# Block-sparse attention and MoE: row maxima by pairs of 64-row matmuls, the mask added on VectorE, tokens in natural order

## The chip, the cores and the metric

The kernel runs on one core of one Trainium2 chip. The time is the device time in microseconds of one execution. A core has five engines with queues of their own: TensorE (PE, matmuls, with its weight loads shown apart as PEld), VectorE (DVE), ScalarE (ACT), GpSimd (POOL) and SyncE (SP), which here issues nearly all DMAs. TensorE writes its results to PSUM, eight banks of 512 fp32 numbers for each of 128 partitions; all else lies in SBUF.

## What is computed

Four batches of eight heads, 768 tokens, 64 numbers a head. Attention is masked by blocks of 32 tokens: a query block sees its neighbours, the first and the last block, and three sampled blocks; the first and last query blocks see all. Then two matrix products with an activation between them.

```python
scores = scale * np.matmul(q, k.transpose(0, 1, 3, 2))
...
scores = np.where(mask, scores, -1000000000.0)
scores = scores - np.max(scores, axis=-1, keepdims=True)
attn = np.exp(scores)
attn = attn / (np.sum(attn, axis=-1, keepdims=True) + 1e-09)
return np.matmul(attn, v)
...
h = x @ w_in                      # x: 3072 x 512, w_in: 512 x 2048
g = np.where(pos, h, np.where(neg, 0.0, (h + beta) ** 2 / (4.0 * beta)))
return g @ w_out                  # 2048 x 512
```

Queries and keys are scaled by 8, so the scores are large and the maximum of each row has to be taken off before the exponential.

## The kernel before

**Precision.** TensorE works on fp32 numbers in a rounded form (F32R). Where that is too coarse, a number is split into a rounded high part and a rounded rest, and three products of the four are summed: in the scores (the rest terms in a second matmul, L304), in the values from head 10 on (L335, L336; heads 0 to 9 multiply whole fp32 numbers, L333), and in both MoE layers (L457 to L459, L485 to L487).

**One head** (`head`, L198). The host gives q and k with the 64 numbers of a token along the partitions and the tokens along the columns, in an order where column t*128 + p is token 6p + t (`_columns`, L596, and the mask's indicator rows `ind`, L586, in the same order). `load_qk` brings q and k of a head into one tile of 128 partitions (q in the lower half L, k in the upper half R). `hi` (L216) rounds it on ScalarE, `lo` (L227) takes the rest on VectorE. Then four DMAs on SP's queue move the halves: `hi_one` (L223) fills rows 0-63 of KA and QA; `hi_two` (L230) and `lo_two` (L236) fill the two halves of QB and KB, which hold a high part and a rest each, arranged so that one matmul of 128 rows sums both mixed products.

QA and KA have more rows than these 64: rows 64 to 87 carry the mask (KA: which block a column belongs to; QA: 0 or -2^33 for each key block, made once by `consts`, L119 to L124), rows 96 to 101 carry the row maximum (KA: ones; QA: minus the maximum of the query). So one matmul gives scores with the mask added, and the score matmul of 102 rows (L303) also takes the maximum off.

**The maxima.** For each of six query tiles t and each half kh of the keys, `max_mm` (L263) multiplies 88 rows (q times k, and the mask) into a PSUM bank of 128 queries x 384 keys, and `max_red` (L271) lets VectorE take the maximum over the 384 into a column of `mc`. Twelve such pairs of matmul and reduction make a head. `max_col` (L276) joins the halves, `max_turn` (L280) transposes the six columns on TensorE, and `max_row` (L283) writes them, negated, into QA's rows 96 to 101.

**Scores to values.** For each half of the queries and each of six key tiles: `scores` (two matmuls), `expo` on ScalarE (L308), a split of p (L196 on ScalarE, L316 on VectorE), running sums on GpSimd (L323), and `values`. Then come the denominators, their reciprocals and the products that make x for the MoE.

**Banks.** The eight PSUM banks are `pa` (three buffers), `po`, `hp` and `oa0` to `oa2`. In the first batch's eight heads (`wide`) the MoE does not run yet, and the scores take `oa0`, `oa1` and `hp` in turn while the maxima take `pa` (`RINGS`, L567). From head 8 on scores, maxima, transposes and sums share the three `pa`.

**Order.** Every step is put into a list with a due time by `at(t, ...)`. The unit is a slot, one score tile: 12 slots a head. Offsets come from tables (P, PW, PA; L555 to L565): the moves are due `qs` slots before the head's scores (12.454 for the first batch, 11.825 for the second, 9.647 then), the maxima `m0` (about 7.8) before them and spread over `m1` (5 to 5.6) slots, each reduction `mr` (0.06 to 0.46) after its matmul. The list is sorted (L545) and the program issued in that order, each engine working through its own part in order. The weights of the two MoE layers are converted on the fly from their 64-bit form in the first stages (`convert`, L157, on ScalarE and VectorE), and the MoE of one batch (`moe`, L434) runs beside the attention of the next. The MoE's output is stored by three tiles at once, or for the last one tile by tile (L490 to L504).

Of the kernel before, what the change touches and what calls it, by code (L numbers as in the profile page):

```python
# [8 lines left out]
F32 = mybir.dt.float32  # L9
# [4 lines left out]
ALU = mybir.AluOpType  # L14
AX = mybir.AxisListType
# [3 lines left out]
B, H, S, D = 4, 8, 768, 64  # L19
NB, BLK, NR = 24, 32, 3  # L20
T = 6
HALF = 384
# [5 lines left out]
KM = 64 + NB  # L28
# [9 lines left out]
def body(ctx, tc, qk_t, v, sampled_blocks, moe_w_in, moe_w_out, ind, cm, negd, ident, fold, out):  # L38
    nc = tc.nc
    pool = lambda name, bufs, **kw: ctx.enter_context(tc.tile_pool(name=name, bufs=bufs, **kw))  # L40
    cst = pool("cst", 1)
    ld = pool("ld", 1)
    tp = pool("tp", 1)
    qk = pool("qk", SETS)
    vp = pool("vp", 2)
    pp = pool("pp", 3)
# [8 lines left out]
    psa = pool("psa", 3, space=PSUM)  # L55
# [5 lines left out]
    Q_MOVE = nc.sync  # L61
# [9 lines left out]
    Q_V = nc.sync  # L71

    def f(ap):
        return ap.bitcast(F32)
# [8 lines left out]
    KAt = [cst.tile([128, S], F32R, name=f"KA{i}") for i in range(SETS)]  # L83
    VW = [vp.tile([128, T, 128], F32, name="vn") for _ in range(2)]
    wi = cst.tile([128, 4, 2, FF], F32R, name="wi")

    def consts():
        M = slice(64, KM)
        for i in range(SETS):
            nc.gpsimd.memset(f(QA[i][64:128 if i == 0 else 96]), 0.0)  # L90
        nc.gpsimd.memset(VW[0][:, :, 64:128], 1.0)
        nc.gpsimd.memset(VW[1][:, :, 0:64], 1.0)
        nc.vector.memset(eps, 1e-9)
        nc.vector.memset(half_c, 0.5)
        sraw = cst.tile([128, NR, 2], I32, name="sraw")
        nc.sync.dma_start(out=sraw[M], in_=sampled_blocks.bitcast(I32).rearrange("a (r w) -> a r w", w=2))
        cmt = cst.tile([128, 2 * NB], F32, name="cmt")
        nc.sync.dma_start(out=cmt[M], in_=cm)
        ef = f(cv.tile([128, 512, 2], I32, name="raw", bufs=3).rearrange("p c w -> p (c w)"))[64:KA, 0:S]
        nc.sync.dma_start(out=ef, in_=ind)  # L100
        idf = pp.tile([128, HALF], F32, name="pt")[:, 0:128]
        nc.sync.dma_start(out=idf, in_=ident)
        nc.vector.tensor_copy(out=idr, in_=idf)
        nc.vector.tensor_copy(out=KAt[0][64:KA], in_=ef)
        nc.sync.dma_start(out=nd, in_=negd.rearrange("a (t p) -> a t p", t=T))
        nc.sync.dma_start(out=sel, in_=fold)
        for i in range(1, SETS):
            rounded(nc.gpsimd, KAt[i][64:KA], ef)
        sf = cst.tile([128, NR], F32, name="sf")
        nc.vector.tensor_copy(out=sf[M], in_=sraw[M, :, 0])  # L110
        al = cst.tile([128, NB], F32, name="al")
        nc.vector.tensor_copy(out=al[M], in_=cmt[M, 0:NB])
        for r in range(NR):
            nc.vector.scalar_tensor_tensor(
                out=al[M], in0=cmt[M, NB:2 * NB], scalar=sf[M, r:r + 1], in1=al[M],
                op0=ALU.is_equal, op1=ALU.max)
        mb = cst.tile([128, NB], F32R, name="mb")
        nc.vector.tensor_scalar(out=mb[M], in0=al[M], scalar1=-1.0, scalar2=BIG, op0=ALU.add, op1=ALU.mult)
        for hf in range(2):  # L119
            cs = slice(hf * HALF, (hf + 1) * HALF)  # L120
            pm = psa.tile([128, 512], F32, name="pa")
            nc.tensor.matmul(out=pm[0:NB, 0:HALF], lhsT=mb[M], rhs=KAt[0][64:KM, cs], start=True, stop=True)
            for i in range(SETS):
                (nc.scalar.copy if i else nc.vector.tensor_copy)(out=QA[i][64:KM, cs], in_=pm[0:NB, 0:HALF])  # L124
# [4 lines left out]
    def at(t, fn, *args):  # L129
        plan.append((t, fn, args))  # L130
# [3 lines left out]
    def bank(wide, use="s"):  # L134

        if wide:
            ring = RINGS[use]
            n = turns[use] = turns.get(use, -1) + 1
            name = ring[n % len(ring)]
            if name[0] == "o":  # L140
                return psc.tile([128, DM], F32, name=name)
            if name == "hp":
                return psh.tile([128, 512], F32, name="hp")
        return psa.tile([128, 512], F32, name="pa")
# [43 lines left out]
    L, R = slice(0, 64), slice(64, 128)  # L188

    def rounded(eng, dst, src):  # L190
        if eng is nc.vector:
            eng.tensor_copy(out=dst, in_=src)
        elif eng is nc.gpsimd:
            eng.tensor_scalar(out=dst, in0=src, scalar1=1.0, scalar2=0.0, op0=ALU.mult, op1=ALU.add)
        else:
            eng.copy(out=dst, in_=src)  # L196

    def head(i, n0, b, h, pst):  # L198

        j, e = divmod(h, 2)  # L200
        wide = i < H
        whole = i // 2 in WHOLE
        G = {**P, **PW} if wide else {**P, **PA} if i < 2 * H else P
        o0, o1 = (L, R) if e == 0 else (R, L)
        QAi, KAi = QA[i % SETS], KAt[i % SETS]
        st = {}

        def load(n, src):
            t = st[n] = ld.tile([128, T, D], F32, name=n)
            Q_V.dma_start(out=t, in_=src[b, h].rearrange("(p t) d -> p t d", t=T))  # L210

        def load_qk():
            st["x"] = ld.tile([128, S], F32, name="qk")
# [6 lines left out]
        def move(dst, src):  # L220
            Q_MOVE.dma_start(out=f(dst), in_=f(src))
# [8 lines left out]
        def hi_two():  # L230
            st["KB"] = qk.tile([128, S], F32R, name="KB")
            st["QB"] = qk.tile([128, S], F32R, name="QB")
            move(st["QB"][L], st["hi"][L])
            move(st["KB"][R], st["hi"][R])

        def lo_two():  # L236
            Q_MOVE.dma_start(out=f(st["QB"][R]), in_=st["x"][L])
            Q_MOVE.dma_start(out=f(st["KB"][L]), in_=st["x"][R])

        def split(pl, n, src, hi, lo):  # L240
            t = st[n] = pl.tile([128, T, 128], F32R, name="vn")
# [7 lines left out]
        pre = n0 - EARLY  # L249
        at(-99 if i == 0 else pre - G["qs"] - G["ld"], load_qk)  # L250
        at(n0 - G["vs"] - G["ld"], load, "lv", v)
        if whole:
            at(n0 - G["vw"], v_whole)
# [2 lines left out]
        at(pre - G["qs"] - 0.4, hi)  # L256
        at(pre - G["qs"] + 0.2, hi_one)
        at(pre - G["qs"] + 0.4, lo)
        at(pre - G["qs"] + 1.3, hi_two)
        at(pre - G["qs"] + 1.6, lo_two)  # L260


        def max_mm(t, kh):  # L263
            if "mc" not in st:
                st["mc"] = pr.tile([128, T, 2], F32, name="mc", bufs=2)
            pm = bank(wide, "m")
            nc.tensor.matmul(out=pm[:, 0:HALF], lhsT=QAi[0:KM, t * 128:(t + 1) * 128],  # L267
                             rhs=KAi[0:KM, kh * HALF:(kh + 1) * HALF], start=True, stop=True)
            st["pm", t, kh] = pm

        def max_red(t, kh):  # L271
            nc.vector.reduce_max(out=st["mc"][:, t, kh:kh + 1], in_=st.pop(("pm", t, kh))[:, 0:HALF], axis=AX.X)  # L272

        def max_col(lo=0, n=T):
            mr = st["mr"] = pr.tile([128, T], F32R, name="mr", bufs=2)
# [8 lines left out]
                                    in0=st["pr"][0:n, 0:128].unsqueeze(1).to_broadcast([n, n - lo, 128]),  # L284
                                    in1=nd[0:n, lo:n], op=ALU.mult)

        jobs = [(t, kh) for t in range(T) for kh in range(2)]
        for n, (t, kh) in enumerate(jobs):
            u = pre - (G["m0"] - G["m1"] * n / len(jobs))
            at(u, max_mm, t, kh)  # L290
            at(u + G["mr"], max_red, t, kh)
        if i == 0:
            for d, fn in ((-0.9, max_col), (-0.89, max_turn), (-0.88, max_row)):
                at(pre - (G["m0"] - G["m1"] / 2) + G["mr"] + H0 + d, fn, 0, T // 2)
# [103 lines left out]
        for hf in range(2):  # L398
# [9 lines left out]
            u = s - 1 + G["lag"]  # L408
# [25 lines left out]
    def moe(t0, p, b, hf, first):  # L434

        g = {}
        G = {**P, **PM} if first else P
# [49 lines left out]
            nc.tensor.matmul(out=o, lhsT=gl[:, ts], rhs=w[:, 0], start=False, stop=(fi == NF - 1))  # L487

        end = b == B - 1 and hf == 1
        dst = out[b * S:(b + 1) * S].rearrange("(p t) m -> p t m", t=T)  # L490

        def o_copy(t):
            if t == 0:
# [12 lines left out]
        for fi in range(NF):  # L506
            u = t0 + fi * p
# [7 lines left out]
            m = u + p / 2  # L515
# [10 lines left out]


    at(TC, consts)
    for i in range(NHEADS):
        b, h = divmod(i, H)  # L530
        if h % 2 == 0:
            pst = {}
        head(i, PER * i, b, h, pst)
    begin = [PER * H * (b + 1) + DELAY for b in range(B + 1)]
    p = PER * H / (2 * NF)
# [39 lines left out]
CONV, CSTEP = 8.0, 5.75  # L575
CLO, CHI = (struct.unpack("<f", struct.pack("<I", w))[0] for w in (0x38100000, 0x47EFFFFF))

_INS = ["qk_t", "v", "sampled_blocks", "moe_w_in", "moe_w_out"]
_OUTS = [((B * S, DM), "float32")]


def _constants():
    import numpy as np

    col = np.arange(S)
    block = (T * (col % 128) + col // 128) // BLK  # L586
    ind = np.concatenate([block[None, :] == np.arange(NB)[:, None], np.zeros((8, S)), np.ones((T, S))]).astype(np.float32)
    i, j = np.arange(NB)[:, None], np.arange(NB)[None, :]
    base = (abs(i - j) <= 1) | (i == 0) | (j == 0) | (i == NB - 1) | (j == NB - 1)
    cm = np.concatenate([base.astype(np.float32), np.broadcast_to(j, (NB, NB)).astype(np.float32)], axis=1)  # L590
    negd = -(np.arange(S)[None, :] // 128 == np.arange(T)[:, None]).astype(np.float32)
    return {"ind": ind, "cm": np.ascontiguousarray(cm), "negd": np.ascontiguousarray(negd),
            "ident": np.eye(128, dtype=np.float32), "fold": np.tile(np.eye(32, dtype=np.float32), (4, 1))}


def _columns(_np, a):  # L596

    return a.reshape(B, H, 128, T, D).transpose(0, 1, 4, 3, 2).reshape(B, H, D, S)


# [27 lines left out]
```

## Time and profile before

| | |
|---|---|
| time, three runs | 981.95, 982.35, 989.32 us (median 982.35) |
| profiled execution | 983.67 us, span 981.8 us |
| busy: TensorE matmul / weight loads | 942.5 us (96%) / 828.1 us (84%) |
| busy: VectorE / ScalarE / GpSimd | 747.5 us (76%) / 636.5 us (65%) / 251.8 us (26%) |
| matmuls and weight loads | 4687 each, 384 of them for the maxima (L267) |
| granted TensorE clock | 0.998 |
| DMA | 154.43 MB, mean 157 GB/s |

The span goes from the first to the last instruction. A matmul's end is modelled and matmuls follow each other in a pipeline, so their durations overlap and a busy TensorE isn't the same as a TensorE at its limit: the pace is read from the starts. A row of a group has the line, the engine, the operation, the tile written and the tiles read, the shapes and the count, then busy time and the mean duration of one in ns, then the idle time before these instructions and what ended it. A row of a timeline has the start in us, the duration in us, the engine, the line and the operation. A row of windows has the stretch, its length, and busy time with count for each engine, then the granted clock, the DMA share and GB/s.

### The profile page before, as it was taken

How to read it: one execution, taken by the hardware profiler on the slowest of the kernel's cores; microseconds unless marked ns; L12 is line 12 of the kernel's file. 1: busy time of each engine (PE TensorE's matmuls, PEld its weight loads, DVE VectorE, ACT ScalarE, POOL GpSimd, SP SyncE). 2: the span in 40 equal slices, each digit the busy share in tenths (PEclk: the TensorE clock that was granted, in tenths of full speed). 3: DMA queues.
4: the chain of work that ended last, by engine and by line, in shares of the span. 5: the costliest groups of instructions: out<-in, count | busy, mean ns of one | idle time of the engine just before them, and what ended most of it. 6: DMA issues, size and time to landing. Idle time of an engine off the chain costs nothing.

```text
span 981.8 us, 14556 instructions
## 1 busy us (share of the span) xinstructions
PE 942.5 (96%) x4687; PEld 828.1 (84%) x4687; DVE 747.5 (76%) x1403; ACT 636.5 (65%) x1302; POOL 251.8 (26%) x229
## 2 busy tenths in 40 slices
PE   5899899999889999999999999999999999999998
PEld 3666677877779899999989998998999999899997
DVE  5888999889998888978788888888888885422222
ACT  3667777677667676767677767776767676433433
POOL 1000000023334343433434343343434343000000
PEclk9999999999999999999999999999999999999999
DMA  6756677754355444645555443645445432433432
GB/s 195 205 149 189 196 209 225 259 180 139 123 182 163 145 143 133 182 139 153 159 150 182 131 150 116 199 137 175 138 142 178 125 115 89 154 130 129 160 129 97
DMA packets 56216, 154.43 MB, mean 157 GB/s; under 512 B 9612, under 2 KB 17952, under 8 KB 56140
## 3 DMA queue, kind: packets, MB, share of 16 engines
q1 hardware_dynamic: 56100, 153.48, 51.5%
q8 instruction: 37, 0.61, 0.3%
q14 instruction: 39, 0.32, 0.1%
q10 hardware_dynamic: 40, 0.03, 0.0%
HBM read 100.92 MB, written 14.81 MB: 118 GB/s over the span
## 4 chain that ended last, share of the span: by engine, by line
PE 85%; DVE 7%; ACT 3%; DMA 2%; issue 2%; SPq 0%; ACTq 0%; DVEq 0%
PE oa L485 8%; PE oa L487 8%; PE oa L486 8%; PE hp L457 8%; PE hp L459 7%; PE hp L458 7%; PE pa L267 7%; PE pa L303 5%; PE pa L304 5%; PE po L335 5%; PE po L336 4%; PE po L333 4%; DVE mc L272 2%; PE oa L333 2%; DMA QA<-qkh 1%
## 5 line engine op out<-in xcount | busy, mean ns | idle before, releaser
L323 POOL TENSOR_TENSOR acc<-acc,pt 128x384 f32<-128x384 f32 x176 | 201.7, 1146 | 233.0 <-ACT pt L308 195.1
L272 DVE TENSOR_REDUCE mc<-pa 128x1 f32<-128x384 f32 x384 | 202.5, 547 | 19.3 <-PE pa L267 16.1
L196 ACT CAST ph<-pt 128x384 fp32r<-128x384 f32 x264 | 135.5, 514 | 92.4 <-PE po L335 89.3
L316 DVE TENSOR_TENSOR pl<-pt,ph 128x384 fp32r<-128x384 f32 x264 | 163.6, 620 | 34.7 <-ACT ph L196 34.0
L308 ACT ACTIVATE pt<-pa 128x384 f32<-128x384 f32 x288 | 140.6, 489 | 54.6 <-PE pa L304 45.0
L457 PE MATMUL hp<-x,wi 128*128 128x384 f32 x448 | 155.5, 347 | 4.0 <-DVE r L469 4.0
L485 PE MATMUL oa<-w,gh 128*128 128x512 f32 x384 | 153.3, 399 | 0.3 <-ACT gh L196 0.3
L487 PE MATMUL oa<-w,gl 128*128 128x512 f32 x384 | 151.6, 395 | 0.3 <-DVE gl L478 0.3
L459 PE MATMUL hp<-x,wi 128*128 128x384 f32 x448 | 151.2, 338 | 0.0
L458 PE MATMUL hp<-x,wi 128*128 128x384 f32 x448 | 151.1, 337 | 0.0
L486 PE MATMUL oa<-w,gh 128*128 128x512 f32 x384 | 150.8, 393 | 0.0
L267 PE MATMUL pa<-KA,QA 88*128 88x384 f32 x384 | 138.3, 380 | 5.4 <-DMA QA<-qkh 3.8
L323 POOL TENSOR_TENSOR acc<-pt 128x384 f32<-128x384 f32 x44 | 46.5, 1058 | 345.5 <-ACT pt L308 345.5
L469 DVE SCALAR_TENSOR_TENSOR r<-r,hp 128x384 f32<-128x384 f32 x112 | 61.5, 549 | 73.3 <-ACT r L466 72.9
L478 DVE TENSOR_TENSOR gl<-r,gh 128x384 fp32r<-128x384 f32 x128 | 84.3, 658 | 24.0 <-ACT gh L196 23.5
L303 PE MATMUL pa<-QA,KA 102*128 102x384 f32 x288 | 99.0, 344 | 1.8 <-ACT pt L308 1.1
L463 ACT ACTIVATE r<-hp,half_c 128x384 f32<-128x384 f32 x112 | 65.1, 582 | 54.1 <-PE hp L459 51.2
L304 PE MATMUL pa<-QB,KB 128*128 128x384 f32 x288 | 97.9, 340 | 0.0
L267 PEld LDWEIGHTS pa<-KA,QA 88*128 88x128 f32 x384 | 73.1, 192 | 28.7 <-DVE mc L272 4.7
L335 PE MATMUL po<-ph,vn 128*128 128x384 f32 x264 | 91.4, 346 | 5.1 <-DVE xun L345 3.4
L457 PEld LDWEIGHTS hp<-x,wi 128*128 128x128 f32 x448 | 84.5, 189 | 10.7 <-DVE r L469 6.1
L336 PE MATMUL po<-pl,vn 128*128 128x384 f32 x264 | 88.6, 336 | 0.0
(97 smaller groups left out, 1624.3 us busy)
## 6 DMA issues: line engine op xcount, KB each, us to landing
w<-wo_dram SPq DMA_DIRECT2D x112, 512.0 KB
qk<-in_qk_t_dram SPq DMA_DIRECT2D x32, 384.0 KB
raw<-in_moe_w_in_dram SPq DMA_DIRECT2D x16, 512.0 KB
raw<-in_moe_w_out_dram SPq DMA_DIRECT2D x16, 512.0 KB
wo_dram<-w SPq DMA_DIRECT2D x16, 512.0 KB
lv<-in_v_dram SPq DMA_DIRECT2D x32, 192.0 KB
KA<-qkh SPq DMA_DIRECT2D x32, 192.0 KB
QA<-qkh SPq DMA_DIRECT2D x32, 192.0 KB
```

Source lines behind the costliest of these rows:

```text
L267: nc.tensor.matmul(out=pm[:, 0:HALF], lhsT=QAi[0:KM, t * 128:(t + 1) * 128], rhs=KAi[0:KM, kh * HALF:(kh + 1) * HALF], start=True, stop=True)
L272: nc.vector.reduce_max(out=st["mc"][:, t, kh:kh + 1], in_=st.pop(("pm", t, kh))[:, 0:HALF], axis=AX.X)
L303: nc.tensor.matmul(out=ps[:, 0:HALF], lhsT=KAi[0:KA, ks], rhs=QAi[0:KA, cs], start=True, stop=False)
L304: nc.tensor.matmul(out=ps[:, 0:HALF], lhsT=st["KB"][:, ks], rhs=st["QB"][:, cs], start=False, stop=True)
L316: (nc.gpsimd if i < 2 * H and c in PL1 else nc.vector).tensor_tensor(out=pl, in0=st["p", c], in1=f(st["ph", c]), op=ALU.subtract)
L323: nc.gpsimd.tensor_tensor(out=st["acc", hf], in0=prev, in1=st["p", c], op=ALU.add)
L457: nc.tensor.matmul(out=hv, lhsT=wi[:, j, 0, fs], rhs=x[:, 0], start=(j == 0), stop=False)
L458: nc.tensor.matmul(out=hv, lhsT=wi[:, j, 0, fs], rhs=x[:, 1], start=False, stop=False)
L459: nc.tensor.matmul(out=hv, lhsT=wi[:, j, 1, fs], rhs=x[:, 0], start=False, stop=(j == NP - 1))
L485: nc.tensor.matmul(out=o, lhsT=gh[:, ts], rhs=w[:, 0], start=(fi == 0), stop=False)
L486: nc.tensor.matmul(out=o, lhsT=gh[:, ts], rhs=w[:, 1], start=False, stop=False)
L487: nc.tensor.matmul(out=o, lhsT=gl[:, ts], rhs=w[:, 0], start=False, stop=(fi == NF - 1))
```

## The change

- **Maxima.** `max_mm` now issues two matmuls of 64 rows one after the other for each query tile: the first for the first half of the keys from rows 0-63 (QA and KA, as before but without the mask rows), the second for the other half of the keys from rows 64-127, with q from the upper half of QB and k straight from the rounded tile `hi`. Each writes a `pa` bank of its own. `max_red` replaces the reduction by one instruction that adds the mask to the 384 numbers, writes the sums back into the same bank, and takes their maximum into `mc`. The mask comes from a table `mq` in SBUF, 128 queries x 6 tiles x 24 key blocks, each entry repeated over a block's 32 keys by the access pattern. Pairs are due every m1/6 slots, the two reductions `mr` and `mr` + m1/12 after the pair.
- **The table.** `consts` makes `mq` by six small matmuls into one bank and a copy on VectorE, ahead of the mask rows of QA, which stay (the score matmul still uses them).
- **Natural order.** Column c is token c. The indicator rows, the host's layout of q, k and v, and the output's store follow. A block of 32 queries is now 32 neighbouring columns.
- **Halves of QB and KB.** The high part of q goes to the upper half of QB and that of k to the lower half of KB, the rests to the others. `hi_two` is due 0.3 slots after the mark instead of 1.3.
- **Buffers.** `tp`, which holds the rounded tile `hi`, has two buffers instead of one.

```diff
-    tp = pool("tp", 1)
+    tp = pool("tp", 2)
...
+    mq = cst.tile([128, T, NB], F32, name="mq")
...
+        pm = psa.tile([128, 512], F32, name="pa")
+        for t in range(T):
+            nc.tensor.matmul(out=pm[:, t * NB:(t + 1) * NB], lhsT=KAt[0][64:KM, t * 128:(t + 1) * 128], rhs=mb[M],
+                             start=True, stop=True)
+        nc.vector.tensor_copy(out=mq, in_=pm[:, 0:T * NB].rearrange("p (t j) -> p t j", j=NB))
...
-            Q_V.dma_start(out=t, in_=src[b, h].rearrange("(p t) d -> p t d", t=T))
+            Q_V.dma_start(out=t, in_=src[b, h])
...
-            move(st["QB"][L], st["hi"][L])
-            move(st["KB"][R], st["hi"][R])
+            move(st["QB"][R], st["hi"][L])
+            move(st["KB"][L], st["hi"][R])
...
-            Q_MOVE.dma_start(out=f(st["QB"][R]), in_=st["x"][L])
-            Q_MOVE.dma_start(out=f(st["KB"][L]), in_=st["x"][R])
+            Q_MOVE.dma_start(out=f(st["QB"][L]), in_=st["x"][L])
+            Q_MOVE.dma_start(out=f(st["KB"][R]), in_=st["x"][R])
...
-        at(pre - G["qs"] + 1.3, hi_two)
+        at(pre - G["qs"] + 0.3, hi_two)
...
-        def max_mm(t, kh):
+        def max_mm(t):
             if "mc" not in st:
                 st["mc"] = pr.tile([128, T, 2], F32, name="mc", bufs=2)
-            pm = bank(wide, "m")
-            nc.tensor.matmul(out=pm[:, 0:HALF], lhsT=QAi[0:KM, t * 128:(t + 1) * 128],
-                             rhs=KAi[0:KM, kh * HALF:(kh + 1) * HALF], start=True, stop=True)
-            st["pm", t, kh] = pm
+            ts = slice(t * 128, (t + 1) * 128)
+            for kh, (q, k, rows) in enumerate(((QAi, KAi, L), (st["QB"], st["hi"], R))):
+                pm = st["pm", t, kh] = bank(wide, "m")
+                nc.tensor.matmul(out=pm[:, 0:HALF], lhsT=q[rows, ts], rhs=k[rows, kh * HALF:(kh + 1) * HALF],
+                                 start=True, stop=True)
 
         def max_red(t, kh):
-            nc.vector.reduce_max(out=st["mc"][:, t, kh:kh + 1], in_=st.pop(("pm", t, kh))[:, 0:HALF], axis=AX.X)
+            pm = st.pop(("pm", t, kh))[:, 0:HALF].rearrange("p (j b) -> p j b", b=BLK)
+            mask = mq[:, t, kh * NB // 2:(kh + 1) * NB // 2].unsqueeze(2).to_broadcast([128, NB // 2, BLK])
+            nc.vector.tensor_tensor_reduce(out=pm, in0=pm, in1=mask, scale=1.0, scalar=-3.0e38, op0=ALU.add,
+                                           op1=ALU.max, accum_out=st["mc"][:, t, kh:kh + 1])
...
-        jobs = [(t, kh) for t in range(T) for kh in range(2)]
-        for n, (t, kh) in enumerate(jobs):
-            u = pre - (G["m0"] - G["m1"] * n / len(jobs))
-            at(u, max_mm, t, kh)
-            at(u + G["mr"], max_red, t, kh)
+        for t in range(T):
+            u = pre - (G["m0"] - G["m1"] * t / T)
+            at(u, max_mm, t)
+            for kh in range(2):
+                at(u + G["mr"] + kh * G["m1"] / 12, max_red, t, kh)
...
-        dst = out[b * S:(b + 1) * S].rearrange("(p t) m -> p t m", t=T)
+        dst = out[b * S:(b + 1) * S].rearrange("(t p) m -> p t m", t=T)
...
-    block = (T * (col % 128) + col // 128) // BLK
+    block = col // BLK
...
-    return a.reshape(B, H, 128, T, D).transpose(0, 1, 4, 3, 2).reshape(B, H, D, S)
+    return a.transpose(0, 1, 3, 2)
...
+    inputs["v_t"] = inputs["v"].reshape(B, H, T, 128, D).transpose(0, 1, 3, 2, 4)
```

More of the change, by code (lines that the diff above doesn't have):

```diff
@@ L576 @@
 CLO, CHI = (struct.unpack("<f", struct.pack("<I", w))[0] for w in (0x38100000, 0x47EFFFFF))
-_INS = ["qk_t", "v", "sampled_blocks", "moe_w_in", "moe_w_out"]
+_INS = ["qk_t", "v_t", "sampled_blocks", "moe_w_in", "moe_w_out"]
 _OUTS = [((B * S, DM), "float32")]
```

## The prediction, made before the run

> **What bounds the kernel now.** I read the table of windows first, because one share for the span hides stages with different limits: the start, the first heads, the transition to the MoE, the steady part and the tail.
>
> ```profile
> 12.00:28.00 16.00, 15.09 (x51) 11.11 (x50) 12.69 (x26) 8.21 (x17) 0.00 (x0) 1.00 0.78 231
> 28.00:165.00 137.00, 126.96 (x519) 92.28 (x519) 122.92 (x243) 94.93 (x191) 0.00 (x0) 0.99 0.65 188
> 165.00:284.00 119.00, 109.42 (x528) 91.78 (x527) 108.38 (x193) 79.88 (x162) 26.99 (x23) 1.00 0.55 181
> 284.00:804.00 520.00, 516.29 (x2716) 475.74 (x2716) 438.32 (x821) 369.02 (x773) 207.17 (x184) 1.00 0.52 152
> 804.00:982.00 178.00, 173.33 (x878) 156.48 (x876) 60.72 (x112) 80.98 (x157) 14.10 (x13) 1.00 0.37 125
> ```
>
> The columns after the length are PE, weight loads, VectorE (DVE), ScalarE and GpSimd busy, then granted clock (0.99 to 1.00), DMA share and GB/s. From 284 on TensorE leaves almost nothing (516 of 520) and VectorE has 82 us to spare. Before 284 VectorE is busy 123 of 137 and 108 of 119 us: there both engines are near their limits, and spare PE time buys little. Second the groups of lines, for the work that the change touches:
>
> ```profile
> L272 DVE TENSOR_REDUCE mc<-pa 128x1 f32<-128x384 f32 x384 | 202.5, 547 | 19.3 <-PE pa L267 16.1
> L267 PE MATMUL pa<-KA,QA 88*128 88x384 f32 x384 | 138.3, 380 | 5.4 <-DMA QA<-qkh 3.8 <-ACT pt L308 1.4 <-DVE mc L272 0.2
> L345 DVE TENSOR_TENSOR xun<-po,otmp 64x384 f32<-64x384 f32 x44 | 24.3, 552 | 1.9 <-ACT otmp L340 0.3
> L276 DVE TENSOR_TENSOR mr<-mc 128x6 fp32r<-128x6 f32 x32 | 5.7, 177 | 0.0
> L94 DVE MEMSET half_c<- 128x1 f32 x1 | 0.1, 59 | 0.0
> ```
>
> Durations overlap, so third the timeline, for the pace. TensorE in the steady part, then VectorE there, then VectorE in the second head:
>
> ```profile
> 401.76 0.34 PE L267 MATMUL pa<-KA,QA 88*128 88x384 f32 x1
> 401.94 0.34 PE L303 MATMUL pa<-QA,KA 102*128 102x384 f32 x1
> 402.12 0.34 PE L304 MATMUL pa<-QB,KB 128*128 128x384 f32 x1
> 402.30 0.40 PE L485 MATMUL oa<-w,gh 128*128 128x512 f32 x1
> ...
> 401.38 0.55 DVE L272 TENSOR_REDUCE mc<-pa 128x1 f32<-128x384 f32 x1
> 401.85 0.55 DVE L316 TENSOR_TENSOR pl<-pt,ph 128x384 fp32r<-128x384 f32 x1
> 402.31 0.55 DVE L272 TENSOR_REDUCE mc<-pa 128x1 f32<-128x384 f32 x1
> 402.78 0.55 DVE L478 TENSOR_TENSOR gl<-r,gh 128x384 fp32r<-128x384 f32 x1
> ...
> 29.31 5.85 DVE L272 TENSOR_REDUCE mc<-pa 128x1 f32<-128x384 f32 x12
> ```
>
> A matmul of 384 columns shows 0.34 us but the next starts 0.18 later (401.76, 401.94, 402.12): it costs 0.18, and 384 maxima cost 67 us of TensorE. A reduction shows 0.55 but the next instruction starts after 0.465. In head 1 twelve reductions run in a row for 5.85 us. Fourth the chain that ended last, in order of time, which says where VectorE itself is on the path:
>
> ```profile
> 12.14 2.89 DVE mc L272 x6
> 29.40 5.77 DVE mc L272 x12
> 114.51 1.49 DVE mc L272 x3
> ```
>
> **The change, part by part.**
>
> *The matmuls.* Twelve of 88 rows a head become six pairs, A in rows 0-63 and B in rows 64-127. Two in sequence cost 0.35 today. The end below: both stream together, 0.18. The end above, without concurrency: 0.35. What lies between is the weight load, and the one place where loads set the pace shows its price:
>
> ```profile
> 169.80 0.34 PE L459 MATMUL hp<-x,wi 128*128 128x384 f32 x1
> 169.80 0.08 PEld L280 LDWEIGHTS pa<-idr,mr 128*6 128x6 f32 x1
> 169.97 0.22 PE L280 MATMUL pa<-idr,mr 128*6 128x128 f32 x1
> 169.98 0.19 PEld L457 LDWEIGHTS hp<-x,wi 128*128 128x128 f32 x1
> 170.04 0.39 PE L457 MATMUL hp<-x,wi 128*128 128x384 f32 x1
> 170.09 0.19 PEld L458 LDWEIGHTS hp<-x,wi 128*128 128x128 f32 x1
> 170.26 0.34 PE L458 MATMUL hp<-x,wi 128*128 128x384 f32 x1
> ```
>
> Loads follow each other after 0.11 at best (169.98, 170.09), and each begins when the matmul before it begins. If B's load may go right behind A's, both take 0.22 beside a preceding matmul of 0.18: the pair costs 0.18 + 0.04 = 0.22. If it may only begin when A's matmul does, B starts 0.11 late and the pair costs 0.29. I take 0.23, nearer the first: a gain of 0.12 a pair.
>
> The Trainium skill (TensorEngine Tiling (Array Packing), Tiling Modes, Key Properties) says that a change of tiling mode drains TensorE. The rows above speak against it as far as they go: the compiled program of before gives L280 a tile of 128 x 32, and the matmul before it is followed after 0.17 and the load behind it after 0.01 us. No row shows a tile of 64 rows. With no drain the sum stays as it is; with one it is the last rival.
>
> *The banks.* A pair needs two "pa" banks at once, of three that the scores use too from head 8 on. How long they are held:
>
> ```profile
> 402.99 0.34 PE L267 MATMUL pa<-KA,QA 88*128 88x384 f32 x1
> 403.37 1.09 DVE L272 TENSOR_REDUCE mc<-pa 128x1 f32<-128x384 f32 x2
> 404.23 0.34 PE L303 MATMUL pa<-QA,KA 102*128 102x384 f32 x1
> 404.40 0.34 PE L304 MATMUL pa<-QB,KB 128*128 128x384 f32 x1
> 404.84 0.49 ACT L308 ACTIVATE pt<-pa 128x384 f32<-128x384 f32 x1 [0.16 <-PE pa L304]
> ...
> 28.00:165.00 137.00, 53.44 (x108) 0.99 0.65 188
> 165.00:284.00 119.00, 19.84 (x37) 1.00 0.55 181
> 284.00:760.00 476.00, 110.23 (x204) 1.00 0.53 155
> ```
>
> The last three rows count L272 alone: 204 in 476 us, so 28 us a head and 2.33 a slot of the plan (12 slots a head). A score holds its bank from 404.23 to 405.33, 1.1 us. The due times put a pair every 0.83 slot (1.94 us), and the second maximum of a pair 0.46 + 0.42 = 0.88 slot after it: after the next pair. Where a score has just been issued, one bank is the score's, one the old second maximum's, and B waits for VectorE or is issued behind other matmuls. By the offsets (pairs at -7.83, -7.00, -6.17, -5.33, -4.50, -3.67, scores at whole slots) that touches four of six pairs; some resolve early, so I count three of six gains. Heads 13 to 31 run from 284 on: 19 x 3 x 0.12 = 6.8 us gained. Between 28 and 165 (54 pairs) PE is not the only limit and a third gain, 54/3 x 0.12 = 2.2. Between 165 and 284, none.
>
> *The maxima on VectorE.* A reduction becomes an addition with a maximum, reading the mask from SBUF and writing the sums back to PSUM. No row shows such an instruction or any VectorE write to PSUM. The end below: as today (L345, PSUM and SBUF, 552 beside L272's 547), extra 0. The end above: an addition and then a reduction, extra 0.465. Nearest I see L345 and beside it the separate writing of one column, between L94's 0.06 and L276's 0.18: extra 0.10. By stage: at the start 6 in the chain, 0.6; 28 to 165, 108 reductions, 10.8 us for an engine with 14 to spare, in bursts that fill it (29.31), half on the path, 5.4; 165 to 284, 37 of them, 3.7, of which 2.2 on the path; from 284, 228 of them, 22.8 us, hidden by the 82 spare us beside TensorE's own work. If that cover fails, the second rival holds.
>
> *The moves.* QB and KB are moved a slot sooner, and B waits for QB where before only scores did. Each head still issues the same four moves on SP. After the start they are due 1.2 to 4.4 slots before the first maximum, so nothing. At the start the chain waits for QA until 11.3 us (below); QB lands behind it: between 0 and another 3 us, taken as 0.8.
>
> ```profile
> 5.36 5.96 DMA QA<-qkh
> ```
>
> *Natural order, mask table, second buffer for the rounded q and k.* Loads keep their bytes; an output store has runs of 2 KB for 6 KB, off the path but for the last, whose rows are 2 KB already. The six small matmuls and the copy for the table lie before 11.3 us, while the move is awaited. Nothing for all; without that cover about 1 us.
>
> The sum: 0.6 + 0.8 + 5.4 + 2.2 - 2.2 - 6.8 = 0.0 against the profiled execution's 983.67 (span 981.8 and 1.9 around it), which lies 1.3 above the median of 982.35. I give 983.
>
> **The rivals.**
>
> *All pairs run together.* The second maximum comes early enough and the banks are there. For it: VectorE has 16% to spare from 284 on. Against: three banks. With 0.19 a pair, 114 x 0.16 = 18.2 and half of 54 x 0.16 = 4.3 are gained, and an extra of 0.06 on VectorE costs 5: 983.7 - 17.5 = 966. The Trainium skill (TensorE: Matmul & The Clock Gate, Part 3) has tiles start about 4 ns after each other; no run here shows it.
>
> *VectorE becomes the bound before 284* (the other side). If the fused instruction costs 0.2 more, 28 to 165 asks for 21.6 with 14 to spare: some 15 on the path; 165 to 284 7.4, 6 on the path; the start 2; from 284 VectorE is at 484 of 513 and half of the gain is left, 3.4: +19.6, 1003. It decides from an extra of about 0.15. For it: the chain already runs through L272 there. Against: the nearest rows.
>
> *No concurrency.* The pairs cost 0.35 and the losses stay: +9, 993, within 1%.
>
> *Drains.* A matmul's tail, 0.34 - 0.18 = 0.16, is exposed at both changes of mode: a pair at 0.23 + 0.32 costs 0.20 more than today: 114 x 0.20 = 23, a third of 72 pairs 5, and VectorE's 9: 1020.
>
> **How the numbers follow.** Forecast 0.30, all together 0.26, VectorE 0.25, no concurrency 0.10, drains 0.09. About 1% is what a measurement of this kernel can tell from no change. Faster by more is the second case, 0.26; within 1% the first and fourth, 0.40; slower the third and last, 0.34. The forecast's own range is 974 to 993. The range runs from 960 (pairs at 0.18, VectorE's extra near 0) to 1010 (an extra of some 0.23), leaving out the drains and the far ends.
>
> **What would show it.** Right: pairs whose starts lie within 0.05 to 0.11 us and a next matmul 0.22 to 0.29 after A; some pairs split by other matmuls or a wait for L272's successor; VectorE's maxima at a pace near 0.57; 28 to 165 some 3 us longer, 284 to 804 some 7 shorter. Wrong: a pace of 0.65 or more, or pairs always 0.35 apart.

## The result and the profile after

The changed kernel takes 1031.86 us (median of six runs, 1030.34 to 1035.39), the kernel before 983.18 in the runs beside it: a ratio of 1.0495, 95% interval 1.0475 to 1.0516. It is 5% slower, outside the predicted range of 960 to 1010. The profiled execution has a span of 1033.6 us where before had 981.8.

Where the 52 us lie is read best by stages that are the same work in both kernels, from the first score matmul of one head to that of another (us, from the starts of L303 in the trace of before and of the same line in the others; the last four rows are experiments, below; each row is one profiled execution):

```text
                          to head 0  0 to 1  1 to 9  9 to 13  13 to 31  31 to end
before                       16.7     20.5   135.6    130.3     506.4    172.2
after                        17.3     24.5   145.6    143.4     530.6    172.3
88 rows, fused instruction   17.3     21.2   130.7    134.6     512.1    172.7
88 rows, plain maximum       16.6     20.8   128.0    133.8     509.1    172.7
64 rows, single, old kernel  15.3     25.2   154.3    142.9     587.9    172.3
64 columns added, old k.     18.2     20.3   140.4    133.1     544.0    172.0
```

Every stage that has maxima grew, and the tail, which has none, did not. Before head 13 the granted clock falls to about a half for a few us at a time (0.51 from 305 to 312 in the changed kernel; in before 0.66 from 38 to 43), not as often in one execution as in another, and a stage there can differ by 2 to 3 us through it (an estimate, half of 3.4 to 6.8 us). From head 13 to 31 the clock is 1.00 in both. In the steady part a head takes 1.34 us more (24.2 over 18 heads), that is 0.22 for each of its six pairs. The windows of the changed kernel at the same places as in the prediction show where to look:

```profile
28.00:165.00 137.00, 130.05 (x461) 74.61 (x460) 116.62 (x316) 87.06 (x175) 0.00 (x0) 0.99 0.60 176
165.00:284.00 119.00, 112.53 (x501) 85.10 (x500) 102.10 (x226) 76.71 (x153) 18.25 (x16) 0.99 0.53 173
284.00:804.00 520.00, 513.51 (x2560) 428.24 (x2559) 439.41 (x991) 350.22 (x734) 195.97 (x174) 0.99 0.50 146
```

From 284 to 804 TensorE looks as busy as before (514 of 520 us for 516), but it issued 2560 matmuls for 2716, and the weight loads fell from 476 to 428 us. The busy time of matmuls hides it, since their modelled ends (0.34 us for a pace of 0.18) cover the gaps between starts; a weight load shows 0.18 to 0.19 us, about one pace, so the share of the loads gives it away. VectorE is as busy as before; whether it is part of the cause is tested below.

One pair in the steady part, in the timeline of TensorE and its weight loads:

```profile
461.70 0.40 PE L496 MATMUL oa<-w,gh 128*128 128x512 f32 x1
461.93 0.40 PE L497 MATMUL oa<-w,gl 128*128 128x512 f32 x1
462.25 0.18 PEld L275 LDWEIGHTS pa<-KA,QA 64*128 64x128 f32 x1 [0.37 <-issue]
462.26 0.44 PE L275 MATMUL pa<-KA,QA 64*128 64x384 f32 x1
462.26 0.18 PEld L275 LDWEIGHTS pa<-qkh,QB 64*128 64x128 f32 x1
462.26 0.44 PE L275 MATMUL pa<-qkh,QB 64*128 64x384 f32 x1
462.62 0.19 PEld L313 LDWEIGHTS pa<-QA,KA 102*128 102x128 f32 x1 [0.18 <-DVE psum L368]
462.63 0.44 PE L313 MATMUL pa<-QA,KA 102*128 102x384 f32 x1
462.73 0.19 PEld L314 LDWEIGHTS pa<-QB,KB 128*128 128x128 f32 x1
462.90 0.34 PE L314 MATMUL pa<-QB,KB 128*128 128x384 f32 x1
```

The pair does what it was made for: both loads and both matmuls start at the same time. But look at the loads. In the stretches quoted before, nearly every load begins when the matmul ahead of it begins. Here the first load waits until L497 has streamed its 512 columns (461.93 + 0.23 = 462.16; 0.23 is their pace, from 461.70 to 461.93) and 0.09 more; the load takes 0.11 in the open, the columns 0.17; then L313's load waits until 462.62, about 0.09 after the columns are through, and takes 0.11 in the open as well. L313's own columns start at 462.73, one pace (0.175) before L314's start. From 462.16 to 462.73 the pair costs 0.57 us, where two 88-row matmuls cost 0.35. Counted in this way, 0.57 is also the median of the 114 pairs that are issued together after 284. For matmuls the profile gives starts alone: that load and columns lie end to end here is read from the matmuls' 0.44 us, 0.10 above the usual 0.34. "Issue" as the reason of the wait means that nothing that the profile shows was waited for. Behind L313's load it names L368, whose tile L313 doesn't read; such a name is no cause.

In the first heads the two halves of a pair are often not issued together, since the three banks aren't free at once. A half then stands alone or meets a half of the next pair:

```profile
48.60 0.44 PE L275 MATMUL pa<-KA,QA 64*128 64x384 f32 x1
48.97 0.45 PE L313 MATMUL oa<-QA,KA 102*128 102x384 f32 x1
49.26 0.34 PE L314 MATMUL oa<-QB,KB 128*128 128x384 f32 x1
49.43 0.81 PE L343 MATMUL po<-ph,vn 128*128 128x384 f32 x2
50.17 0.44 PE L275 MATMUL pa<-qkh,QB 64*128 64x384 f32 x1
50.17 0.44 PE L275 MATMUL pa<-KA,QA 64*128 64x384 f32 x1
50.45 0.33 PE L275 MATMUL pa<-qkh,QB 64*128 64x384 f32 x1
```

The half at 48.60 is a run of its own; its partner follows at 50.17, side by side with the first half of the next pair, and that pair's second half comes at 50.45. Before 165 the 54 pairs make 67 runs of 64-row matmuls, and 39 of these are one half alone.

VectorE's part, in the groups of lines and in the timeline of the steady part:

```profile
L281 DVE CUSTOM_DVE_ANT_1 pa<-pa,mq 128x384 f32<-128x384 f32 x384 | 209.6, 572 | 43.1 <-PE pa L275 40.9
L281 DVE DVE_READ_ACCUMULATOR2_ANT mc<- 128x1 f32 x384 | 53.8, 140 | 0.0
...
463.47 0.56 DVE L281 CUSTOM_DVE_ANT_1 pa<-pa,mq 128x384 f32<-128x384 f32 x1
463.94 0.14 DVE L281 DVE_READ_ACCUMULATOR2_ANT mc<- 128x1 f32 x1
463.94 0.56 DVE L488 TENSOR_TENSOR gl<-r,gh 128x384 fp32r<-128x384 f32 x1
```

The fused maximum is two instructions in the profile, the second a read of the accumulator with 0.14 us. But the next instruction starts together with that read (463.94), so its 0.14 is not added to the pace: 0.47 to the next start here, against 0.465 in the lines of the plain reduction. Over the two whole traces the median from such an instruction to the next start on VectorE, the read left aside (gaps under 0.7), is 0.483 against 0.468, so 15 ns more.

### The profile page after: what moved, and what is told of

Read it like the earlier page. It is cut to its first block, busy times and chain, and to the rows that moved or that the text cites. A ratio compares the mean times of both kernels' runs of the same rounds, so it can differ in the third digit from the quotient of the medians.

```text
span 1033.6 us, 14940 instructions
## 1 busy us (share of the span) xinstructions
PE 998.4 (97%) x4693; PEld 797.1 (77%) x4693; DVE 775.6 (75%) x1788; ACT 637.5 (62%) x1302; POOL 250.1 (24%) x229
## 4 chain that ended last, share of the span: by engine, by line
PE 90%; DVE 4%; DMA 2%; ACT 2%; issue 1%; SPq 0%; ACTq 0%; DVEq 0%
PE hp L467 9%; PE oa L495 8%; PE pa L275 8%; PE oa L497 8%; PE oa L496 8%; PE hp L468 7%; PE hp L469 7%; PE pa L313 5%; PE po L345 5%; PE pa L314 5%; PE po L343 5%; PE po L346 4%; PE oa L343 3%; PE oa L313 2%; PE oa L314 1%; PE pa L469 1%
## 5 line engine op out<-in xcount | busy, mean ns | idle before, releaser
L333 POOL TENSOR_TENSOR acc<-acc,pt 128x384 f32<-128x384 f32 x176 | 193.6, 1100 | 247.3 <-ACT pt L318 234.3
L281 DVE CUSTOM_DVE_ANT_1 pa<-pa,mq 128x384 f32<-128x384 f32 x384 | 209.6, 572 | 43.1 <-PE pa L275 40.9
L326 DVE TENSOR_TENSOR pl<-pt,ph 128x384 fp32r<-128x384 f32 x264 | 172.0, 651 | 43.1 <-ACT ph L202 40.5
L318 ACT ACTIVATE pt<-pa 128x384 f32<-128x384 f32 x288 | 140.4, 488 | 71.5 <-PE pa L314 58.9
L467 PE MATMUL hp<-x,wi 128*128 128x384 f32 x448 | 163.5, 365 | 4.3 <-DVE r L479 4.3
L468 PE MATMUL hp<-x,wi 128*128 128x384 f32 x448 | 152.5, 340 | 0.0
L469 PE MATMUL hp<-x,wi 128*128 128x384 f32 x448 | 151.8, 339 | 0.0
L497 PE MATMUL oa<-w,gl 128*128 128x512 f32 x384 | 151.7, 395 | 0.0
L333 POOL TENSOR_TENSOR acc<-pt 128x384 f32<-128x384 f32 x44 | 53.0, 1205 | 384.1 <-ACT pt L318 384.1
L313 PE MATMUL pa<-QA,KA 102*128 102x384 f32 x288 | 103.2, 358 | 0.3 <-DVE QA L293 0.2
L467 PEld LDWEIGHTS hp<-x,wi 128*128 128x128 f32 x448 | 84.9, 189 | 22.6 <-issue 11.4
L314 PE MATMUL pa<-QB,KB 128*128 128x384 f32 x288 | 98.6, 342 | 0.0
L488 DVE TENSOR_TENSOR gl<-r,gh 128x384 fp32r<-128x384 f32 x128 | 78.9, 616 | 23.9 <-ACT gh L202 23.6
L275 PE MATMUL pa<-KA,QA 64*128 64x384 f32 x192 | 85.7, 446 | 3.6 <-DMA QA<-qkh 1.7
L468 PEld LDWEIGHTS hp<-x,wi 128*128 128x128 f32 x448 | 85.1, 190 | 2.6 <-DVE mc L281 0.3
```

The source lines that it names most:

```text
L275: nc.tensor.matmul(out=pm[:, 0:HALF], lhsT=q[rows, ts], rhs=k[rows, kh * HALF:(kh + 1) * HALF], start=True, stop=True)
L281: nc.vector.tensor_tensor_reduce(out=pm, in0=pm, in1=mask, scale=1.0, scalar=-3.0e38, op0=ALU.add, op1=ALU.max, accum_out=st["mc"][:, t, k ...
L313: nc.tensor.matmul(out=ps[:, 0:HALF], lhsT=KAi[0:KA, ks], rhs=QAi[0:KA, cs], start=True, stop=False)
L314: nc.tensor.matmul(out=ps[:, 0:HALF], lhsT=st["KB"][:, ks], rhs=st["QB"][:, cs], start=False, stop=True)
L326: (nc.gpsimd if i < 2 * H and c in PL1 else nc.vector).tensor_tensor(out=pl, in0=st["p", c], in1=f(st["ph", c]), op=ALU.subtract)
L333: nc.gpsimd.tensor_tensor(out=st["acc", hf], in0=prev, in1=st["p", c], op=ALU.add)
```

## The experiments

The theory after the result: at both ends of a run of matmuls in tiles of 64 rows, the matmuls ahead have to run out (they drain), and the weights next in line aren't loaded ahead across the change (change of mode). Its rivals were the prediction's other terms: pairs that need two of three banks, and the slower instruction on VectorE.

**88-row maxima, all else as changed.**

```diff
-            for kh, (q, k, rows) in enumerate(((QAi, KAi, L), (st["QB"], st["hi"], R))):
+            for kh, (q, k, rows) in enumerate(((QAi, KAi, slice(0, KM)), (QAi, KAi, slice(0, KM)))):
```

> The changed kernel, but both maxima of a pair are 88-row matmuls again (with the mask rows, as before the change), issued as a pair into two banks; VectorE still adds the mask while it takes the maximum, and all else of the change stays. Theory (change of mode: a pair of 64-row matmuls costs 0.57 us for 0.35, since the matmul ahead of it and the pair itself have to run out and the next weights aren't loaded ahead): nearly all of the loss goes, 983 to 992 us, and in the steady part a pair costs 0.35 again. Rival (three banks for pairs, and the slower instruction on VectorE): both are still there, so it stays above 1015.

Measured: 990.61 us, 1.0084 of before (1.0063 to 1.0105). Of the loss 41 us go with the 64-row tiles alone. A pair, still issued as a pair, in the timeline of the steady part:

```profile
458.70 0.34 PE L314 MATMUL pa<-QB,KB 128*128 128x384 f32 x1
458.88 0.52 PE L275 MATMUL pa<-KA,QA 88*128 88x384 f32 x2
459.24 0.40 PE L495 MATMUL oa<-w,gh 128*128 128x512 f32 x1
```

The pair starts one pace after L314 (458.70, 458.88) and the next matmul 0.36 us later (459.24): no gap on either side. By the same count 100 of 113 such pairs after 284 cost less than 0.45. The rival of banks is out as the main cause, since these pairs need two banks at once as well. It is not nothing: between 284 and 804 the loads of these pairs wait 9.4 us for readers of a `pa` bank (5.5 for ScalarE's L318, 3.9 for VectorE's L281), where the maxima of before wait 2.5 for ScalarE's. So the stage from head 13 to 31 stays 5.7 us longer than before, and the 64-row tiles account for 18.5 of its 24.2 us, 0.17 a pair.

**The plain maximum on the 64-row pairs.** `max_red` is again the reduction of before.

```diff
-            pm = st.pop(("pm", t, kh))[:, 0:HALF].rearrange("p (j b) -> p j b", b=BLK)
-            mask = mq[:, t, kh * NB // 2:(kh + 1) * NB // 2].unsqueeze(2).to_broadcast([128, NB // 2, BLK])
-            nc.vector.tensor_tensor_reduce(out=pm, in0=pm, in1=mask, scale=1.0, scalar=-3.0e38, op0=ALU.add,
-                                           op1=ALU.max, accum_out=st["mc"][:, t, kh:kh + 1])
+            nc.vector.reduce_max(out=st["mc"][:, t, kh:kh + 1], in_=st.pop(("pm", t, kh))[:, 0:HALF], axis=AX.X)
```

> The changed kernel with the 64-row pairs, but VectorE takes the plain maximum as before the change (the mask is left out of the maximum). Theory (change of mode): stays at 1022 to 1032, since VectorE's instruction costs only about 0.02 us more at its pace. Rival (VectorE): falls to 1000 or below.

Measured: 1029.62 us, 1.0483 of before (1.0462 to 1.0504). VectorE's instruction accounts for some 2 us of the 49, no more than the intervals leave open; with the plain maximum nearly all of the loss stays.

**Both matmuls of a pair in the same half.**

```diff
-            for kh, (q, k, rows) in enumerate(((QAi, KAi, L), (st["QB"], st["hi"], R))):
+            for kh, (q, k, rows) in enumerate(((QAi, KAi, L), (QAi, KAi, L))):
```

> The changed kernel, but both matmuls of a pair lie in rows 0 to 63 (of QA and KA), so that the mode changes as often and nothing runs side by side. Theory (change of mode): a pair costs 0.57 + 0.17 = 0.74, 114 x 0.17 = 20 us more in the steady part alone, 1055 to 1065 in all, and it shows what running side by side is worth. If the two do not really run side by side in the changed kernel: no difference from 1032.

Measured: 1056.73 us, 1.0762 of before (1.0744 to 1.078). A run of two, one after the other, in the steady part:

```profile
443.97 0.40 PE L497 MATMUL oa<-w,gl 128*128 128x512 f32 x1
444.29 0.61 PE L275 MATMUL pa<-KA,QA 64*128 64x384 f32 x2
444.83 0.44 PE L313 MATMUL pa<-QA,KA 102*128 102x384 f32 x1
445.11 0.34 PE L314 MATMUL pa<-QB,KB 128*128 128x384 f32 x1
```

Counted in the same way, from 443.97 + 0.23 = 444.20 to 445.11 - 0.175 = 444.94, it is 0.74 where the pair side by side has 0.57. So running side by side is real and worth 0.17 in the lines; the change of mode takes 0.40 for it. In time it is worth less: heads 13 to 31 take 543.9 us, 13.3 more than with pairs side by side or 0.12 a pair, where I expected some 20 in the steady part. What covers the rest was not traced.

**88 rows and the plain maximum.** The first two edits together: only natural order, the table, the halves, the sooner move, the second buffer and issuing by twos remain.

> The changed kernel with the maxima as before the change in both respects (88-row matmuls with the mask rows, plain maximum), still issued by twos; natural order, the table, the halves of QB and KB, the sooner move and the second buffer stay. All theories of the maxima: 983 within 5 us. Against the run with 88 rows and the fused instruction it gives that instruction's price alone: by the pace 0 to 4 us, by the prediction's 0.10 each about 8.

Measured: 984.51 us, 1.0013 of before (0.9993 to 1.0032): no difference. Against the first experiment the fused instruction costs 6.1 us, 16 ns each, which agrees with the 15 ns of the pace. The rest of the change, taken together, costs nothing that can be told.

**64-row matmuls in the kernel before.**

```diff
-            nc.tensor.matmul(out=pm[:, 0:HALF], lhsT=QAi[0:KM, t * 128:(t + 1) * 128],
-                             rhs=KAi[0:KM, kh * HALF:(kh + 1) * HALF], start=True, stop=True)
+            nc.tensor.matmul(out=pm[:, 0:HALF], lhsT=QAi[L, t * 128:(t + 1) * 128],
+                             rhs=KAi[L, kh * HALF:(kh + 1) * HALF], start=True, stop=True)
```

> The kernel before, with one edit: each of the twelve matmuls for the maxima reads rows 0 to 63 only (the mask is left out of the maximum). No pairs, no fused instruction, no change of order. Theory (change of mode): each of them that stands alone between 128-row matmuls costs 0.57 for 0.18 us, 228 x 0.39 = 89 us in the steady part, and less before it, where several follow each other: 1075 to 1110. Rival (the loss came from pairing and banks): 983.

Measured: 1102.41 us, 1.1211 of before (1.117 to 1.1251). One edit, fewer rows, less work, and 119 us more: this shows the price of the tile without pairs, fused instruction or new order. A single one costs what a pair costs:

```profile
427.16 0.40 PE L487 MATMUL oa<-w,gl 128*128 128x512 f32 x1
427.49 0.18 PEld L267 LDWEIGHTS pa<-KA,QA 64*128 64x128 f32 x1 [0.36 <-DVE pl L316]
427.49 0.43 PE L267 MATMUL pa<-KA,QA 64*128 64x384 f32 x1
427.85 0.19 PEld L335 LDWEIGHTS po<-ph,vn 128*128 128x128 f32 x1 [0.18 <-issue]
427.86 0.45 PE L335 MATMUL po<-ph,vn 128*128 128x384 f32 x1
427.96 0.19 PEld L336 LDWEIGHTS po<-pl,vn 128*128 128x128 f32 x1
428.14 0.34 PE L336 MATMUL po<-pl,vn 128*128 128x384 f32 x1
```

From 427.16 + 0.23 to 428.14 - 0.175 is 0.57 again. Heads 13 to 31 grew by 81.5 us for 216 maxima, 0.38 each; the theory said 0.39.

**Each pair twice.** After the two matmuls of a pair the same two are issued again into the same banks.

```diff
-                nc.tensor.matmul(out=pm[:, 0:HALF], lhsT=q[rows, ts], rhs=k[rows, kh * HALF:(kh + 1) * HALF],
-                                 start=True, stop=True)
+            for again in range(2):
+                for kh, (q, k, rows) in enumerate(((QAi, KAi, L), (st["QB"], st["hi"], R))):
+                    nc.tensor.matmul(out=st["pm", t, kh][:, 0:HALF], lhsT=q[rows, ts], rhs=k[rows, kh * HALF:(kh + 1) * HALF],
+                                     start=True, stop=True)
```

> The changed kernel with each pair of 64-row matmuls issued twice in a row into the same banks (the second run writes the same numbers). Theory (the mode's cost is paid once for a run of matmuls in one mode): the second pair costs 0.17 to 0.18, a run of two pairs 0.75, and the time is 1032 + 20 to 33 = 1052 to 1065. If every 64-row pair costs 0.57 by itself: 1100 or more.

Measured: 1053.16 us, 1.071 of before (1.0677 to 1.0743). Within the mode loads go ahead as usual (460.15 for the second pair, which starts at 460.32):

```profile
460.04 0.18 PEld L277 LDWEIGHTS pa<-KA,QA 64*128 64x128 f32 x1 [0.25 <-issue]
460.04 0.44 PE L277 MATMUL pa<-KA,QA 64*128 64x384 f32 x1
460.04 0.18 PEld L277 LDWEIGHTS pa<-qkh,QB 64*128 64x128 f32 x1
460.04 0.44 PE L277 MATMUL pa<-qkh,QB 64*128 64x384 f32 x1
460.15 0.19 PEld L277 LDWEIGHTS pa<-KA,QA 64*128 64x128 f32 x1
460.15 0.19 PEld L277 LDWEIGHTS pa<-qkh,QB 64*128 64x128 f32 x1
460.32 0.34 PE L277 MATMUL pa<-KA,QA 64*128 64x384 f32 x1
460.32 0.34 PE L277 MATMUL pa<-qkh,QB 64*128 64x384 f32 x1
460.59 0.19 PEld L469 LDWEIGHTS hp<-x,wi 128*128 128x128 f32 x1 [0.25 <-issue]
```

The second pair starts 0.28 after the first, of which 0.11 is the first pair's load, so it adds 0.17 (19.7 us for 108 pairs between heads 13 and 31, 0.18 each). The 0.40 is paid once for a run.

**A tile of fewer columns instead.** In the kernel before, ahead of each matmul for the maxima:

```diff
+            nc.tensor.matmul(out=pm[0:64, 0:HALF], lhsT=QAi[0:KM, t * 128:t * 128 + 64],
+                             rhs=KAi[0:KM, kh * HALF:(kh + 1) * HALF], start=True, stop=True)
```

> The kernel before with an extra matmul ahead of each of the 384 for the maxima: the same 88 rows, but 64 of the 128 columns, into the lower half of the same bank, which the full one then overwrites. It tells whether a tile of fewer columns costs what one of fewer rows costs. If only a change of the row tile runs the array empty: an extra matmul costs 0.18, 228 x 0.18 = 40 us in the steady part, 1025 to 1045 in all. If every change of tile does: 0.57 each, 1100 or more.

Measured: 1030.14 us, 1.0476 of before (1.0443 to 1.0508), and 37.6 us for 216 extra matmuls between heads 13 and 31, 0.17 each: their own columns and nothing else. The compiled program gives these matmuls a tile of 128 x 64, so it is the tile that differs and not only the count of columns in use. The load goes ahead as always:

```profile
441.67 0.34 PE L461 MATMUL hp<-x,wi 128*128 128x384 f32 x1
441.67 0.13 PEld L267 LDWEIGHTS pa<-KA,QA 88*64 88x64 f32 x1
441.84 0.34 PE L267 MATMUL pa<-KA,QA 88*64 88x384 f32 x1
441.85 0.19 PEld L269 LDWEIGHTS pa<-KA,QA 88*128 88x128 f32 x1
442.02 0.33 PE L269 MATMUL pa<-KA,QA 88*128 88x384 f32 x1
```

**What of the change is good.** The run with 88 rows and the plain maximum was 7.6 us shorter than before between heads 1 and 9 and 6.2 longer from there to head 31. Four more kernels were run to find the reason. Their stage times come from one execution each, while the time of one kernel varies by 4 to 9 us between executions, so differences of 1 to 3 us in a stage show nothing by themselves. With the maxima of before, one by one, and all else as changed:

> The changed kernel with the matmuls and reductions of the maxima as before the change and due one by one as before, so that natural order, the table, the halves of QB and KB, the sooner move and the second buffer remain. The run that issued 88-row maxima by twos was 7.6 us shorter than before between heads 1 and 9 and 6.2 longer after. If the gain comes from the sooner move or the second buffer and the loss from issuing by twos: 973 to 978. If issuing by twos made both: 980 to 984.

Measured: 983.45 us, ratio 0.9999 (0.9978 to 1.002): the same, with 129.5 us between heads 1 and 9 and 132.5 and 507.5 in the two stages after. The total is in the range for the case that issuing by twos made both, but the gain of 6 us in the first heads is still there, so it isn't from issuing by twos. The kernel before with `tp` at two buffers:

> The kernel before with one edit: two buffers for the rounded tile instead of one. Where the 6 us come from that 88-row maxima in the changed surroundings gain between heads 1 and 9. If from the second buffer: heads 1 to 9 in 128 to 130 us, and 976 to 980 in all. If not: 983.

Measured: 982.96, 1.0005 (0.9992 to 1.0017), 134.8 us there: not the second buffer. The first of these two kernels with `hi_two` back at 1.3 slots:

> The changed kernel with the maxima as before the change, one by one, and the second pair of moves due 1.3 slots after the mark as before the change. If the sooner move made the gain between heads 1 and 9: back to 135 us there. If it made the loss from head 9 on instead: the gain stays, the loss goes, 976 to 980 in all.

Measured: 985.23, 1.002 (1.0006 to 1.0033), 134.6, 130.9 and 506.1 us in the three stages: the gain goes with the sooner move. Whether the small loss later goes with it too is not shown; its difference (1.6 and 1.4 us) is too small for one trace. Then the sooner move for the first batch alone, `at(pre - G["qs"] + (0.3 if wide else 1.3), hi_two)`:

> As the kernel with 88-row maxima one by one, but the second pair of moves is due sooner only in the first eight heads. If both halves of that account hold (sooner is good there, later is good from head 8 on): 974 to 979, faster than before. Otherwise 980 to 985.

Measured: 979.46, 0.9965 (0.9952 to 0.9978), with 130.2, 131.0 and 505.8 us, half a us past the 974 to 979 that I expected. This is the one kernel that is faster than before: 0.35%, with the maxima left alone. The stages are those of its fastest execution (976.28 us). Why the sooner move helps in the first heads was not traced further.

## Why the prediction was wrong

*The step that failed is the price of a pair*, "I take 0.23". It measured 0.57. The sum had the pairs as a gain of 9.0 us (2.2 and 6.8); the 64-row tiles cost 41, and these 50 us make up the 49 by which the time was off. I had two bounds, full overlap and none, 0.18 and 0.35, and left what lies above 0.35 to a rival with a chance of 0.09. That rival, drains, was the mechanism: it put a pair at 0.55 and the total at 1020, and the runs show 0.57 and 1032. That 0.55 is so near is in part luck: it was made of 0.23 for the pair and two tails of 0.16, and the lines show 0.17 for the columns and, at either end, 0.09 of waiting and a load of 0.11 in the open, which the rival didn't have. It came out short before 284, where it counted a third of 72 pairs, some 5 us; between heads 1 and 13 the 64-row tiles alone cost 23.7 us (289.0 against 265.3 with 88 rows), since there halves issued apart make runs of their own. In the steady part it had 23 us, and the tiles cost 18.5 there.

*Why the rule was weighed too low.* The Trainium skill (TensorEngine Tiling (Array Packing), Tiling Modes, Key Properties) says that changing the mode drains TensorE. I set L280 against it, whose tile has 32 columns and which drained nothing. That row's starts were read rightly and stretched too far (only "each begins when the matmul before it begins" is not so in those lines for L458's load, at 170.09, 0.05 after L457): the run with 64 columns shows that a tile of fewer columns costs nothing, the runs with 64 rows that a tile of fewer rows costs 0.40 a run of matmuls. For rows the rule holds here; for columns these runs speak against it. A row of the same family was not a row of the same thing, and the range should have reached the drains, since no row excluded them.

*The banks.* Three of six pairs were to be split in the steady part. They aren't: by the starts in the trace 114 of 115 pairs after 284 are issued together. What three banks do cost is waiting: with 88 rows and the plain maximum, issued by twos, the stage from head 13 to 31 is 2.7 us longer than before, and 5.7 with the fused instruction. In the first heads splitting is common: 22 of 54 pairs before 165 are issued together. The term was 6.8 us of gain at most, so it did not decide.

*VectorE.* The extra of 0.10 an instruction was 0.016 (6.1 us over 384), near the end below. That the three terms for it (0.6, 5.4 and 2.2) come near 6.1 in sum is luck: they held half of the extra in the first heads on the path and none from 284 on, and by the traces of the two kernels with 88 rows 3.0 us of it lie between heads 13 and 31. The read of the accumulator exists, with 0.14, but the next instruction doesn't wait for it. The rival with VectorE as the bound fell by this. That the reading is an instruction of its own is what the Trainium skill says (VectorE: DVE Perf Modes, Two Vector instructions with no wait between them), and the trace agrees.

*The moves and natural order.* Priced at 0.8 and nothing; the run with 88 rows and the plain maximum is the same as before within 0.3%. That the sooner move alone gains about 5 us in the first heads was not foreseen.

*What held.* Side by side works, as forecast: in 93 of the 114 pairs after 284 the starts are 3 to 4 ns apart (0.00 to 0.01 in the lines; most of the others 60 ns), which agrees with the Trainium skill's 4 ns (TensorE: Matmul & The Clock Gate, Part 3). And in TensorE's steady part a price per pair counts nearly in full: against the kernel with 88 rows, whose pairs have a median of 0.37, the lines give 0.20 a pair, and the stage grew by 0.17.

## What to carry to other kernels

Count changes of the row tile before counting rows saved: here a run of 64-row matmuls between 128-row ones costs 0.40 us on top of its own columns, and side by side saves 0.17 for each pair by the lines. By these numbers (an estimate, not tried) a run needs three pairs or more in a row to gain, and so six free banks. Where a trace has no row for an operation's mode, the nearest row is no bound; the new tile in the old kernel, one edit, settles it first.

The busy time of matmuls didn't show these gaps (514 of 520 us), the start of the weight load did: where it no longer fell together with the start of the matmul ahead, 0.20 us were lost.

## What the hardware showed that I had not expected

- A run of 64-row tiles between 128-row ones costs two parts at each end: about 0.09 us of waiting after the last columns, and the weight load of 0.11 in the open (461.93 to 462.90 above). What goes on in the array meanwhile, no profile shows.
- Two weight loads for the two halves of the array start together, and so do their matmuls (462.25 and 462.26 above).
- A tile of 64 columns amid full ones costs no change at all: 0.17 us, the pace of 384 columns, and its load shows 0.13 for 0.19.
- A fused addition and maximum that reads PSUM and SBUF, and writes PSUM, has nearly the pace of a plain reduction: 0.483 against 0.468 as medians.
